# Zero products of a two-layer attention and feed-forward kernel: placed by a weighed sum of the product kinds, issued in four column groups, with new letters for the order

## The chip, the cores and the metric

The kernel runs on one core of a Trainium2 chip. The metric is the device time of one execution in microseconds (us). Several executions are timed; one more is profiled, and its profile gives a span (first to last instruction) and the clock that TensorE was granted.

## What is computed

The reference takes one sequence of 2048 rows of 512 bf16 numbers through two equal layers with shared weights. 32 heads have 16 dimensions each, and the hidden width of the feed-forward part is 1792.

```python
x = A_x
x = x + attention(layernorm(x), A_wqkv, A_wo)      # softmax(q k^T / 4) v, 32 heads of 16, full (no mask)
x = x + silu(layernorm(x) @ B_w1) @ B_w2
x = x + attention(layernorm(x), A_wqkv, A_wo)
x = x + silu(layernorm(x) @ B_w1) @ B_w2
```

## The kernel before

**Tiles and segments.** The attention of a layer is cut into segments: a chunk of 512 queries and a block of four heads (`Seg`). A segment runs over key tiles of 128 keys, and a key tile over two pairs of heads, which makes 2048 tiles in all. TensorE computes the scores of a tile with two matmuls of 32 rows (L1282, in the scores function) into one of three PSUM slots of 128 x 1024. Then one of two engines takes the exponential of the slot:

- ACT does it directly in one instruction of 128 x 1024 (L1497, `act_turn`).
- DVE writes a linear function of the score as 16-bit bits (L1531, `dve_turn`), and three shifted copies of it are made, each by one pass on POOL (L1592, `pool_turn`) or on DVE (L1565). The four together stand for one exponential, so such a tile feeds TensorE four value products instead of one.

The value product (L1358, `values`) has 17 stationary columns (16 dimensions and a column of ones for the sum) and writes into one 32-partition group of the PSUM tile `o_ps`. Two or four of them stand side by side in the array's column groups.

**Side work.** The projections to keys, queries and values, the output projection and the feed-forward part are lists of steps (`Piece`). Their products are issued as four matmuls of 32 columns side by side (L312). The hidden layer's activation is a tanh on ACT (L580) with a DVE instruction behind it (L584). A query tile `QT` needs a chain: the maximum of the keys (L348, L355), a bias matrix `bm` (L412), the absolute query `qu` (L404), one product of the two (L312) and a sum (L421). Without `QT` no scores of its segment can be issued.

**The order.** Everything between the opening and the ending is put in order by a planner that runs while the program is built (`Flow`). It keeps a clock for PE, ACT, DVE and POOL, with fixed durations for each instruction, and gives the next turn to the engine whose clock is earliest. PE has two modes: R for scores, in which the array is split in row groups, and C for values and side work, in which it is split in column groups. Each change between them is planned at 100 ns (`SWITCH`), a product step at 217 ns (`MM`). The engines then run in the recorded order. `due` in the planner says when ACT will need the next scores.

**The letters.** For each stretch of 16 tiles a letter of `RULES` picks seven settings from `KINDS` (`rule`, L977): how many buffers must be free for DVE to take a tile, how many value pairs may wait before they go ahead of side work, at how few free buffers they go anyway, how many shift passes may wait when DVE takes another tile, a factor on the pace of the side work, and from which length of the queue and with which wait DVE helps with passes.

**Zero products.** If PE has nothing to issue that fits ahead of the next scores, `pe_turn` calls `warm` (L1379). Here a matmul of zero weights (16 columns of `wkq` that hold zeros) may be issued. It adds nothing to `o_ps`, or writes into a bank or slot that nobody uses at that time. It is issued only when the share of the last 3300 ns in which PE was planned to stream (`share`, L1375) is at most `WARM`, 0.65, or `HOT`, 0.9, while the next tile has no query tile yet. In mode R it uses 32 rows, in mode C 128 rows, and it always uses one column group. The opening (L1736) and the ending (L660) have zero products of their own.

Of the kernel before, what the change touches and what calls it, by code (L numbers as in the profile page):

```python
# [20 lines left out]
def kernel(  # L21
# [10 lines left out]
    nc = tc.nc  # L32
# [3 lines left out]
    S, D = xf.shape  # L36
    F = B_w1.shape[-1]
    P = 128
    H = 32
    DH = D // H  # L40
# [8 lines left out]
    KR = 32  # L49
# [890 lines left out]
    class Flow:  # L940
# [114 lines left out]
        def step(self, p, at):  # L1055

            engine, ns, fn, g = p.steps.pop(0)
            if not p.begun and p not in self.bg:
                self.cur = p
                for q in self.qs:  # L1060
                    if p in q:
                        q.remove(p)
            p.begun = True
            if p.chain is not None:
                self.chain = p.chain
            self.credit -= ns
            if engine == "pe":
                if self.mode != "C":
                    at += SWITCH
                self.mode = "C"  # L1070
                end = self.pe = at + ns
                self.runs.append((at, end))
                lat = (0, 200, 200)
            elif engine == "dve":
                if "l" in g:
                    at = max(at, self.lock)
                    self.held_port = at + ns
                end = self.dve = at + ns
                lat = (50, 0, 50)
            else:  # L1080
                self.act = max(at + ns, self.end - 446)
                self.end = max(at + ns + 113, self.end + 491)
                end = self.end
                lat = (50, 32, 0)
            fn()
            if p.store is not None and turns:
                p.store.done = True
                p.store.ready = self.landed(end)
            if p.steps:
                p.land = max(p.land, self.landed(end))  # L1090
            if g == "c":
                self.g = end + 50
                self.cur = None
                if p.steps:
                    self.bg.append(p)
            if p.steps:
                p.ready = end + lat[("pe", "dve", "act").index(p.steps[0][0])]
            else:
                p.done = True
                if p.chain is not None and p.chain["last"] is p:  # L1100
                    self.chain = None
                p.ready = max(p.land, self.landed(end), end + 50 + p.lag)
                if p in self.bg:
                    self.bg.remove(p)
# [155 lines left out]
        def scores(self, at, picks):  # L1260

            if self.mode != "R":
                at += SWITCH
            self.mode = "R"
            two = len(picks) == 2
            self.pe = at + (MM + 8 if two else MM + 3)
            self.runs.append((at, at + MM))
            new = []
            for k in picks:
                t = Tile(self.n)  # L1270
                if self.n % STRETCH == 0:
                    self.rule(self.n)
                self.n += 1
                if t.seg.i > self.started:
                    self.started = t.seg.i
                    self.begin(t.seg)
                if t.pr == 0 and t.kt != t.seg.kts[0]:
                    self.pace(t.seg, t.kt - t.seg.kts[0])
                t.slot, t.at = k, at
                for jj in range(2):  # L1280
                    j = 2 * t.pr + jj
                    nc.tensor.matmul(  # L1282
                        self.slots[k][:, jj, :],
                        lhsT=KT[32 * j : 32 * j + KR, t.seg.hb, t.kt * P : (t.kt + 1) * P],
                        rhs=t.seg.QT[32 * j : 32 * j + KR, :],
                        start=True,
                        stop=True,
                    )
                self.held[k] = t
                new.append(t)  # L1290
            if two and len(self.lanes[new[0].pr]) < len(self.lanes[new[1].pr]) - EVEN:
                new.reverse()
            for t in reversed(new):
                if self.want_dve(t, at, two) and not any(x.dve for x in new):
                    t.dve = True
                    self.last_dve = t.n
                    self.zs.append(t)
                    t.bufs = [self.take()] + [None] * (len(SHIFTS) - 1)
            self.exps += sorted((t for t in new if not t.dve), key=lambda t: t.n)
# [43 lines left out]
        def values(self, at, rows):  # L1343

            if self.mode != "C":
                at += SWITCH
            self.mode = "C"
            self.pe = at + MM + 4
            self.runs.append((at, at + MM))
            seg = segs[self.open]  # L1350
            for r in rows:
                _, t, buf, term = r
                pr = t.pr
                self.lanes[pr].remove(r)
                seg.rows[pr] -= 1
                for jj in range(2):
                    j = 2 * pr + jj
                    nc.tensor.matmul(  # L1358
                        self.o_ps[32 * j : 32 * j + VW, :],
                        lhsT=vs[seg.L][:, t.kt, 4 * seg.hb + j, :],  # L1360
                        rhs=buf[:, jj, :],
                        start=not seg.opened[pr],
                        stop=seg.rows[pr] == 0,
                        skip_group_check=True,
                    )
                seg.opened[pr] = True
                t.uses[term] -= 1
                if not t.uses[term]:
                    self.give((self.pe + 150, buf))
            if seg.rows == [0, 0]:  # L1370
                self.close_at = self.pe + 204

        def share(self, t):  # L1375
            self.runs = [r for r in self.runs if r[1] > t - SPAN]
            return sum(b - max(a, t - SPAN) for a, b in self.runs) / SPAN

        def warm(self, t, limit):  # L1379
            idle = self.n < len(tiles) and tiles[self.n][0].QT is None  # L1380
            if t + MM > limit or self.share(t) > (HOT if idle else WARM):
                return False
            if any(segs[self.open].opened) and self.close_at is None:
                out = self.o_ps
            elif self.cur is None and self.g <= t:
                out = narrow("w_ps")
            else:
                slots = [k for k in range(3) if self.held[k] is None and self.free[k] <= t]
                if not idle or not slots:
                    return False  # L1390
                out = self.slots[slots[0]][:, 0, :]
            rows = slice(0, KR if self.mode == "R" else P)
            nc.tensor.matmul(  # L1393
                out[0:DH, :], lhsT=wkq[rows, 0, 2 * D : 2 * D + DH], rhs=wo_sb[rows, 0, :],
                start=out is not self.o_ps, stop=out is not self.o_ps, skip_group_check=True,
            )
            self.pe = t + MM
            self.runs.append((t, self.pe))
            return True


# [57 lines left out]
        def tail(self, t):  # L1459
            if self.n < len(tiles) or not self.units or not self.turned.done:  # L1460
                return False
            tq, k = self.units[0]
            if len(self.kept) <= tq // 2:
                free = [
                    i for i in range(3)
                    if self.held[i] is None and self.free[i] <= t and i not in self.kept
                ]
                if not free:
                    return False
                self.kept.append(free[0])  # L1470
            if self.mode != "C":
                t += SWITCH
            self.mode = "C"
            tail_mm([self.slots[i] for i in self.kept], tq, k)
            self.units.pop(0)
            self.pe = t + MM
            self.runs.append((t, self.pe))
            return True

        def act_turn(self):  # L1480
# [135 lines left out]
    SWITCH, T_PASS, T_BITS, T_SHIFT = 100, 1225, 430, 1000  # L1616

    LAST, ROWS, LATE, EVEN = 5, 20, 900, 0
    SPAN, WARM = 3300, 0.65
    STRETCH = 16  # L1620
    KINDS = {
# [10 lines left out]
    }  # L1632
    RULES = (
        "bbbbbbbbmmmmmmmmwwwwwwwwwwwwwwwwppppppppbbbbbbbbddddddddcccccccc"
        "aaaaaaaakkkkkkkknnnnnnnnvvvvvvvvwwwwwwwwwwwwwwwweeeeeeeellllllll"
    )
    TAU, NEAR, URGENT, HARD = 700, 300, 4000, 6000
    FROM, TO, EARLY = 0, 99, 300
    EARLIER = 12
    SOON, CLOSE = 150, -9999  # L1640
    HOT = 0.9
    MOST = 2600

    OPENING = """
# [6 lines left out]
    at = {}  # L1651
# [142 lines left out]
```

## Time and profile before

| what | value |
|---|---|
| median of 3 runs | 1627.8 us (1621.85, 1627.8, 1628.68) |
| profiled execution | 1620.71 us, of which the span is 1618.9 us |
| mean granted TensorE clock | 0.991 |
| busy PE, DVE, ACT, POOL | 1546.3, 1239.8, 1557.0, 1293.6 us |
| exponentials on ACT, on DVE | 1596, 452 |
| zero products in the trace, L1393 | 211 |

A busy time counts every moment in which at least one instruction of the engine is under way. Matmuls overlap each other in the pipeline, so a PE that is always busy isn't at its peak. Rows of the timeline merge instructions of one kind that follow each other, with their count behind an x. "Idle before" is the time in which the engine did nothing ahead of such a row, with the instruction whose end released it.

### The profile page before, as it was taken

To read this page: it belongs to the slowest core of one execution; us is meant where nothing else is said; L and a number is where in the kernel's file an instruction comes from. 1 tells how busy PE (TensorE), PEld (TensorE's weight loads), DVE (VectorE), ACT (ScalarE), POOL (GpSimd) and SP (SyncE) were. 2 spreads that over 40 slices of the span, in tenths; PEclk is the share of its full clock that TensorE was granted. 3 is DMA by queue.
4 is the path that set the end of the run, shared out by engine and by line. 5 is a ranking of instruction groups with operands and counts; after the bars stand their busy time and mean duration, and the time that the engine had idled before them with its cause. 6 is when DMAs were issued, how large, how long until landed. Compare 5 with 4: busy or idle time off the path is not lost.

```text
span 1618.9 us, 41459 instructions
## 1 busy us (share of the span) xinstructions
PE 1546.3 (96%) x16750; PEld 477.4 (29%) x16756; DVE 1239.8 (77%) x1550; ACT 1557.0 (96%) x1767; POOL 1293.6 (80%) x1349
## 2 busy tenths in 40 slices
PE   8999999999999999999999999998999999999998
PEld 3322222233322323233222232222223222222333
DVE  7898888876777678658987668886878887777764
ACT  6999999999999999999999998998999999999993
POOL 3899998987898778868777866876879998889880
PEclk9999999999999999999999999998999999999999
DMA  5011101100210011001120011112100110010000
GB/s 195 21 40 37 30 23 27 27 11 11 37 23 11 11 27 41 11 14 33 57 59 23 14 27 35 37 35 45 30 11 17 33 27 14 18 33 18 17 24 14
DMA packets 105744, 49.24 MB, mean 30 GB/s; under 512 B 79024, under 2 KB 105040, under 8 KB 105552
## 3 DMA queue, kind: packets, MB, share of 16 engines
q1 hardware_dynamic: 103536, 45.51, 11.0%
q8 instruction: 131, 2.15, 0.6%
q10 hardware_dynamic: 2016, 1.08, 0.2%
q14 instruction: 61, 0.50, 0.1%
HBM read 17.20 MB, written 11.27 MB: 18 GB/s over the span
## 4 chain that ended last, share of the span: by engine, by line
PE 59%; ACT 22%; DVE 11%; issue 6%; POOL 2%; DMA 1%; ACTq 0%; DVEq 0%; POOLq 0%
PE slot L1282 21%; PE q_ps L1358 19%; ACT p L1497 15%; PE y_ps L312 7%; PE h_ps L312 4%; DVE p L1531 3%; ACT v L1497 3%; ACT t_sb L580 2%; PE k_ps L312 2%; PE v_ps L312 1%; PE q_ps L312 1%; POOL p L1592 1%; DVE hT L584 1%; PE w_ps L1393 1%; DVE kq L334 1%
## 5 line engine op out<-in xcount | busy, mean ns | idle before, releaser
L1497 ACT ACTIVATE p<-slot 128x1024 bf16<-128x1024 f32 x1168 | 1172.4, 1203 | 17.4 <-PE slot L1282 17.1
L1592 POOL TENSOR_TENSOR p<-p,steps 128x512 int32<-128x512 int32 x681 | 710.9, 1068 | 186.6 <-DVE p L1531 167.2
L1282 PE MATMUL slot<-QT,KT 32*128 32x512 bf16 x4096 | 596.6, 383 | 36.8 <-ACT p L1497 18.3
L1358 PE MATMUL q_ps<-p,v 128*17 128x512 bf16 x4956 | 566.1, 384 | 5.6 <-DVE p L1531 2.3
L1531 DVE TENSOR_SCALAR p<-slot 128x1024 uint16<-128x1024 f32 x341 | 415.5, 1219 | 106.0 <-PE slot L1282 99.9
L1282 PEld LDWEIGHTS <-KT 32*128 32x128 bf16 x4096 | 198.8, 91 | 615.9 <-issue 609.9
L1497 ACT ACTIVATE v<-slot 128x1024 bf16<-128x1024 f32 x289 | 329.3, 1211 | 1.9 <-PE slot L1282 1.9
L1358 PEld LDWEIGHTS <-v 128*17 128x17 bf16 x6808 | 157.3, 88 | 292.9 <-issue 244.1
L1358 PE MATMUL q_ps<-v,v 128*17 128x512 bf16 x1222 | 195.2, 382 | 1.2 <-POOL v L1592 0.8
L1592 POOL TENSOR_TENSOR v<-p,steps 128x512 int32<-128x512 int32 x159 | 170.4, 1081 | 23.2 <-DVE p L1531 17.1
L1592 POOL TENSOR_TENSOR p<-v,steps 128x512 int32<-128x512 int32 x123 | 130.8, 1081 | 8.4 <-DVE v L1531 8.0
L312 PE MATMUL h_ps<-xnT,w_sb 128*32 128x512 bf16 x1568 | 130.3, 384 | 6.8 <-DVE hT L584 6.6
L312 PE MATMUL y_ps<-w_sb,hT 128*32 128x512 bf16 x1568 | 121.8, 383 | 0.5 <-DVE hT L584 0.5
L584 DVE SCALAR_TENSOR_TENSOR hT<-t_sb,h_ps 128x512 bf16<-128x512 f32 x98 | 66.8, 682 | 58.2 <-ACT t_sb L580 57.9
L1531 DVE TENSOR_SCALAR v<-slot 128x1024 uint16<-128x1024 f32 x69 | 84.2, 1220 | 26.8 <-PE slot L1282 25.7
L1497 ACT ACTIVATE wkq<-slot 128x1024 bf16<-128x1024 f32 x74 | 87.2, 1215 | 0.1
L312 PE MATMUL k_ps<-xnT,wkq 128*32 128x512 bf16 x960 | 78.2, 383 | 0.0
L580 ACT ACTIVATE t_sb<-h_ps 128x512 f32<-128x512 f32 x98 | 76.0, 776 | 0.0
L421 DVE SCALAR_TENSOR_TENSOR QT<-qc,cols,q_ps 128x512 bf16<-128x512 bf16 x74 | 55.0, 743 | 21.6 <-PE q_ps L312 21.0
L1358 PE MATMUL q_ps<-wkq,v 128*17 128x512 bf16 x336 | 58.3, 387 | 0.6 <-ACT wkq L1497 0.4
L312 PEld LDWEIGHTS <-hT 128*32 128x32 bf16 x2016 | 41.0, 95 | 57.1 <-issue 40.8
L1497 ACT ACTIVATE wv_sb<-slot 128x1024 bf16<-128x1024 f32 x44 | 51.7, 1174 | 4.7 <-PE slot L1282 4.5
(168 smaller groups left out, 1469.5 us busy)
## 6 DMA issues: line engine op xcount, KB each, us to landing
qc<-kept_q SPq DMA_DIRECT2D x70, 112.0 KB, 2.0
kept_q<-kq SPq DMA_DIRECT2D x60, 128.0 KB, 1.8
w_sb<-in_B_w_dram SPq DMA_DIRECT2D x2, 1792.0 KB, 13.0
out_dram<-x_sb SPq DMA_DIRECT2D x15, 128.0 KB, 1.7
x_sb<-in_A_x_dram SPq DMA_DIRECT2D x3, 512.0 KB, 7.0
old_q<-QT SPq DMA_DIRECT2D x10, 128.0 KB, 1.7
q_was<-old_q SPq DMA_DIRECT2D x10, 128.0 KB, 2.0
at<-oT SPq DMA_TRANSPOSE x63, 2.3
```

What stands on the lines that cost most here:

```text
L312: nc.tensor.matmul(ps[g, :], lhsT=lhsT[:, g], rhs=rhs, start=start, stop=stop, skip_group_check=True)
L334: nc.vector.tensor_copy(out=st[:], in_=cell["ps"][:, :])
L421: nc.vector.scalar_tensor_tensor(out=dst, in0=qc[:], scalar=own, in1=ps, op0=ALU.mult, op1=ALU.add)
L580: nc.scalar.activation(t_sb, ps, ACT.Tanh, scale=0.5)
L584: nc.vector.scalar_tensor_tensor(out=hT[:, ft, :], in0=t_sb, scalar=1.0, in1=ps, op0=ALU.add, op1=ALU.mult)
L1282: nc.tensor.matmul(self.slots[k][:, jj, :], lhsT=KT[32 * j : 32 * j + KR, t.seg.hb, t.kt * P : (t.kt + 1) * P], rhs=t.seg.QT[32 * j : 32 * ...
L1358: nc.tensor.matmul(self.o_ps[32 * j : 32 * j + VW, :], lhsT=vs[seg.L][:, t.kt, 4 * seg.hb + j, :], rhs=buf[:, jj, :], start=not seg.opened ...
L1393: nc.tensor.matmul(out[0:DH, :], lhsT=wkq[rows, 0, 2 * D : 2 * D + DH], rhs=wo_sb[rows, 0, :], start=out is not self.o_ps, stop=out is not ...
L1497: nc.scalar.activation(buf[:].rearrange("p a b -> p (a b)"), self.slots[x.slot][:].rearrange("p a b -> p (a b)"), ACT.Exp, scale=float(SCALE),
L1531: nc.vector.tensor_scalar(out=whole.bitcast(U16), in0=self.slots[x.slot][:].rearrange("p a b -> p (a b)"), scalar1=float(UNIT), scalar2=fl ...
L1592: nc.gpsimd.tensor_tensor(out=b1.bitcast(I32), in0=b0.bitcast(I32), in1=steps32[:, k : k + 1].to_broadcast([P, 512]), op=ALU.add,)
```

## The change

The planner records for each PE step a weight beside its time: `ANY` plus `SCORE`, `VALUE` or `SIDE` for each product that runs side by side in it. The sum of time by weight over the last 3400 ns (`heat`) takes the place of the share, with the bounds 1.4 (`WARM`) and 2.2 (`HOT`). A zero product is now four matmuls of 128 rows in the four column groups. If PE is in mode R, the planner changes to C first and adds 100 ns; only where that doesn't fit ahead of the next scores does it issue a single one of 32 rows. Last, 21 of the 32 groups of four letters in `RULES` are others.

```diff
-                self.runs.append((at, end))
+                self.runs.append((at, end, ANY + 4 * SIDE))
...
-            self.runs.append((at, at + MM))
+            self.runs.append((at, at + MM, ANY + (4 if two else 2) * SCORE))
...
-            self.runs.append((at, at + MM))
+            self.runs.append((at, at + MM, ANY + 2 * VALUE * len(rows)))
...
-        def share(self, t):
+        def heat(self, t):
             self.runs = [r for r in self.runs if r[1] > t - SPAN]
-            return sum(b - max(a, t - SPAN) for a, b in self.runs) / SPAN
+            return sum((b - max(a, t - SPAN)) * w for a, b, w in self.runs) / SPAN
...
-            if t + MM > limit or self.share(t) > (HOT if idle else WARM):
+            if t + MM > limit or self.heat(t) > (HOT if idle else WARM):
...
-            rows = slice(0, KR if self.mode == "R" else P)
-            nc.tensor.matmul(
-                out[0:DH, :], lhsT=wkq[rows, 0, 2 * D : 2 * D + DH], rhs=wo_sb[rows, 0, :],
-                start=out is not self.o_ps, stop=out is not self.o_ps, skip_group_check=True,
-            )
+            narrowly = self.mode == "R" and t + MM + 2 * SWITCH > limit
+            if self.mode == "R" and not narrowly:
+                t += SWITCH
+                self.mode = "C"
+            rows = slice(0, KR if narrowly else P)
+            for j in range(1 if narrowly else 4):
+                nc.tensor.matmul(
+                    out[32 * j : 32 * j + DH, :], lhsT=wkq[rows, 0, 2 * D : 2 * D + DH],
+                    rhs=wo_sb[rows, 0, :],
+                    start=out is not self.o_ps, stop=out is not self.o_ps, skip_group_check=True,
+                )
             self.pe = t + MM
-            self.runs.append((t, self.pe))
+            self.runs.append((t, self.pe, ANY if narrowly else ANY + 4 * SIDE))
...
-    SPAN, WARM = 3300, 0.65
+    SPAN, WARM = 3400, 1.4
+    ANY, SCORE, VALUE, SIDE = 0.9, 0.27, 0.58, 0.47
...
-        "bbbbbbbbmmmmmmmmwwwwwwwwwwwwwwwwppppppppbbbbbbbbddddddddcccccccc"
-        "aaaaaaaakkkkkkkknnnnnnnnvvvvvvvvwwwwwwwwwwwwwwwweeeeeeeellllllll"
+        "mmmmllllllllllllCCCCCCCCCCCCCCCCmmmmmmmmmmmmBBBBvvvvdddddddddddd"
+        "aaaaaaaakkkkkkkknnnnnnnnddddddddwwwwwwwwwwwwwwwwhhhhyyyynnnnaaaa"
...
-    HOT = 0.9
+    HOT = 2.2
```

More of the change, by code (lines that the diff above doesn't have):

```diff
@@ L1476, in tail @@
             self.pe = t + MM
-            self.runs.append((t, self.pe))
+            self.runs.append((t, self.pe, ANY + 4 * SIDE))
             return True
```

## The prediction

> **What bounds the kernel now.** First the page's busy shares and slices.
>
> ```profile
> PE 1546.3 (96%) x16750; PEld 477.4 (29%) x16756; DVE 1239.8 (77%) x1550; ACT 1557.0 (96%) x1767; POOL 1293.6 (80%) x1349
> ...
> ACT  6999999999999999999999998998999999999993
> ...
> PEclk9999999999999999999999999998999999999999
> ```
>
> PE and ACT are equally busy, so the share doesn't tell which one decides. The timeline does: is one of them issued at a fixed step, without gaps?
>
> ```profile
> 700.31 0.60 ACT L580 ACTIVATE t_sb<-h_ps 128x512 f32<-128x512 f32 x1
> ...
> 700.79 1.04 ACT L1497 ACTIVATE p<-slot 128x1024 bf16<-128x1024 f32 x1
> ...
> 702.59 6.57 ACT L1497 ACTIVATE p<-slot 128x1024 bf16<-128x1024 f32 x7
> ...
> 704.04 1.48 PE L312 MATMUL y_ps<-w_sb,hT 128*32 128x512 bf16 x24
> ```
>
> Seven exponentials take 6.57 us and one takes some 1.06, so one follows the other by (6.57 - 1.06) / 6 = 0.918 us; the tanh takes 0.48 of ACT's order (700.31 to 700.79). ACT's first exponential starts at 31.8 us and the last ends at 1576.5: 1544.7 us. At 0.917 and 0.49, 1596 exponentials, 98 tanh and 10 rescaling exponentials (L493) need 1516.4. So **ACT's order is the bound**: 98 % of the main stretch, and the rest is 28.3 us of pauses. The groups put 24.7 us of idle ahead of L1497 (17.4 + 1.9 + 0.1 + 4.7 + 0.6, by output), nearly all ended by scores from PE; the other 3.6 refill ACT's pipeline. PE matters only where scores are late. Its 24 side products are six steps of four, (1.48 - 0.39) / 5 = 0.218 us each.
>
> The second question is the granted clock. In narrow stretches it is 0.5 in five places and 1.0 elsewhere. The next rows are the five stretches of half clock, the 3.41 us ahead of two of them, and one ordinary stretch; columns are PE, PEld, DVE, ACT, POOL busy, then the clock.
>
> ```profile
> 244.98:248.39 3.41, 3.41 (x26) 0.57 (x28) 1.54 (x2) 2.49 (x4) 2.88 (x4) 0.50 0.02 3
> 599.97:603.38 3.41, 3.41 (x23) 0.47 (x22) 2.55 (x3) 2.78 (x3) 3.13 (x4) 0.50 0.14 32
> 1077.83:1084.66 6.83, 6.30 (x46) 1.15 (x44) 4.34 (x7) 5.19 (x6) 3.03 (x3) 0.50 0.43 58
> 1115.38:1125.62 10.24, 9.32 (x52) 1.80 (x50) 5.90 (x8) 4.91 (x6) 5.87 (x7) 0.50 0.10 24
> 1132.45:1135.86 3.41, 3.41 (x31) 0.82 (x34) 2.94 (x5) 2.92 (x4) 2.53 (x3) 0.50 0.10 34
> ```
> ```profile
> 241.57:244.98 3.41, 3.14 (x22) 0.90 (x20) 1.96 (x3) 3.41 (x5) 3.40 (x4) 1.00 0.16 38
> ...
> 1111.97:1115.38 3.41, 2.15 (x16) 0.60 (x16) 2.76 (x4) 3.41 (x4) 3.41 (x4) 1.00 0.00 0
> ...
> 1202.00:1205.41 3.41, 2.95 (x40) 0.83 (x33) 2.24 (x4) 3.41 (x5) 1.35 (x2) 1.00 0.00 0
> ```
>
> The half clock comes in units of 3.41 us, eight in all, 27.3 us. ACT idles there for 0.92 + 0.63 + 1.64 + 5.33 + 0.49 = 9.0 us; with its share of the refills (28.3 / 24.7) that is 10.3 us. The worst place shows how:
>
> ```profile
> 1120.38 0.75 DVE L421 SCALAR_TENSOR_TENSOR QT<-qc,cols,q_ps 128x512 bf16<-128x512 bf16 x1 [3.41 <-PE q_ps L312]
> ...
> 1121.88 1.02 ACT L1497 ACTIVATE wv_sb<-slot 128x1024 bf16<-128x1024 f32 x1 [3.53 <-PE slot L1282]
> ```
>
> The bias product for the next query tile is late at half clock, so QT is, so are the scores, and ACT stands for 3.53 us.
>
> What precedes a drop? Not an idle PE: 3.14 us of 3.41 are busy at 241.57, more than the 2.95 at 1202. It is the number of products in column groups:
>
> ```profile
> 1111.97:1115.38 3.41, 0.99 (x6) 0.19 (x6) 1.00 0.00 0
> ...
> 1202.00:1205.41 3.41, 1.58 (x18) 0.39 (x11) 1.00 0.00 0
> ```
>
> These are the value products (L1358): 6 against 18. With side products and zero products the five stretches ahead of a drop hold 6 to 15, the one at 1202 holds 30. Cutting the whole main stretch into such windows (a product at an edge by its part), 443 have full clock and a median of 28 column products. Of 8 with under 11, four precede a drop; of 18 with under 14, five; of the rest none. So a low count is necessary here and isn't always enough.
>
> **The change, part by part**, by the recorded orders of both programs.
>
> 1. *Exponentials.* ACT gets 1591 instead of 1596; tanh stay 112 (14 of them in the ending). 5 x 0.917 = **-4.6 us** on the bound. What takes them: DVE has 5 more L1531 (1.22 us each) and 6 more passes L1565 (0.77), POOL 9 more L1592 (1.07): 10.7 us of DVE and 9.6 us of POOL, hidden by their idle shares of 23 and 20 %. Without that cover the late values would hold buffers and delay ACT, by 10.7 us at most.
>
> 2. *Zero products in the flow.* 211 steps become 141: 138 of four products and 3 narrow ones. That frees 70 x 0.217 = 15.2 us of PE. Value steps +14, scores steps -9, side steps -2 cost 0.7; six more mode changes each way cost 12 x 0.10 = 1.2 (scores at 703.72 to products at 704.04 is 0.32, less the step of 0.217). PE's order gets 13.3 us shorter, but it isn't the bound. I take 0. The price of a group of four isn't in the trace: like four side products it is one step of 0.218; at worst its four loads of 16 columns (L1393, 86 ns each) stand in a row, 0.344, and 138 x 0.127 = 17.5 us would lie on PE. I take the first, the nearer row. Behind each stands the next score step or value step, and ACT waits only for the first; 67 of the 141 steps stand right ahead of scores, against 107 of 211 before.
>
> 3. *The clock.* Unknown, with two ends: all eight units go (-10.3), or none (0), or more come (below). What the row says: ahead of the drops stood 4, 3, 2, 0 and 3 zero products. Of two thirds as many steps, each four wide, three become two steps and eight products, so a window of 10 gets to 15, above the 14 under which drops occurred. Laid out along ACT's order (0.917 and 0.49 per instruction), windows of 3.41 us with under 11 column products are about 5 in the order before and 1.5 in the order after; with under 14, 19 and 12. That is 0.3 to 0.65 of the risk left. But the window at 1111.97, which cost the most, had no zero product at all: PE stood waiting there, which the planner didn't foresee. I take half: **-5 us**.
>
> 4. *The letters.* They change which scores go to DVE and when side work runs, so ACT's other pauses (24.7 - 9.0 = 15.7 us idle) are drawn anew. The order shows where scores pause: stretches of at least eight column steps between two score steps are 7 before and 12 after. The longest, at tile 1274, goes from 22 steps to 15; before it is ACT's pause of 4.0 us at 992.5, ended by scores after a wait for QT's chain on DVE, which stays, so I count no gain. A new one of 13 steps stands at tile 1026, and the old one of 12 steps at 1050 (1.1 us idle at 814.9) is down to 8. I take 0, with -4 and +10 as ends.
>
> 5. *The ending.* Two products of the output projection move from the flow into it: 2 x 0.22, half hidden behind ACT's copies: +0.2, ends 0 and 0.4. The opening's order is the same.
>
> The sum: 1620.7 - 4.6 - 5 + 0.2 = **1611.3** for an execution like the profiled one (1620.71, of which 1.8 us lie outside the span). That one is 7 us below the median of 1627.8; the four known times stand as two pairs, near 1621 and 1628, mean 1624.8. Since the program is fixed, I put the spread to how many windows drop (an estimate; one execution can't show it). Some of it stays, +1: I predict **1612**, 1.0 % below the median.
>
> **A rule against it.** The Trainium skill, "TensorE: Matmul & The Clock Gate", section "Part 1: The HAM clock gate (the "warmup" mystery)", says that the clock follows how busy PE was in free-running windows of 3413 ns, and that a window of idleness halves it. The units of 3.41 us agree; the idleness doesn't, for PE is 63 to 92 % busy in the two windows shown ahead of drops. By the rule, groups of four gain no more than single products, and the sum is that of rival B; by the row, it is point 3.
>
> **Rivals.**
>
> - *B: busy time decides, not products; or the drops just move.* Then four side by side count like one, the wider groups do nothing, and 70 fewer steps even hurt. For it: the window at 1111.97 is also low in PE busy (2.15 us of 3.41). Against: 3.14 busy dropped, 2.95 did not. It gives 1620.7 - 4.6 = 1616; with a quarter more units (2 x 10.3 / 8 = 2.6), 1619. The rule above leads here.
> - *C: all units go.* 1620.7 - 4.6 - 10.3 = 1606.
> - *D, slower: the new order starves ACT.* Five more long stretches without scores. ACT holds three slots, 2.75 us; eight steps and two changes are 1.95, so they cost nothing if the slots are full, and up to the 4.0 us of tile 1274 if QT is late. Five at 4.0, with no clock gained, are 1620.7 - 4.6 + 20 = 1636. At 2.5 us each it is 0.5 % above the profiled time (1628.8), at 4.0 each 0.5 % above the median (1635.9). For it: 13 steps at tile 1026. Against: the four 8-step stretches that exist (tiles 448, 1138, 1922, 1952) lie in slices in which ACT is busy for 40.0 of 40 us.
>
> **How the numbers follow.** Half mended 0.42 (1612, its own range 1607 to 1617), C 0.17, B 0.25, D 0.16. A measurement can tell about 0.5 %, 8 us. Faster: the forecast, C, and a quarter of B, 0.65. Same: the rest of B and a quarter of D, 0.23. Slower: 0.12. The range reaches to C with a few us of luck in point 4 (1602) and over B to the mild side of D, 1627.
>
> **What would show it.** Right: ACT's step still 0.917 with 1591 exponentials, half clock in under five units, idle ahead of L1497 near 20 us, groups of four in 0.22 steps. Wrong: eight or more units; or new pauses of over 2 us at tile 1026 (some 794 us in the order before) or near the changed letters; or score steps late behind zero products.

## The result, and the profile after

| | before | after |
|---|---|---|
| median of 22 executions | 1624.32 us (1620.03 to 1629.54) | 1620.21 us (1617.32 to 1622.98) |
| ratio of the times, 95 % interval | | 0.9974 (0.9965 to 0.9984) |
| profiled execution | 1620.71 us (span 1618.9) | 1622.98 us (span 1621.2) |
| mean granted clock | 0.991 | 0.993 |
| exponentials on ACT | 1596 | 1591 |

The change saves 4.1 us, 0.26 % (0.16 to 0.35 %). The forecast was 1612, 8 us lower. The two profiled executions alone would say the opposite, 2.3 us slower: the one of before is near the fastest of its 22, the one of after is the slowest of its 22. So one more execution of before was profiled, and two more of after, and stretches are compared by means over all of them.

From the page of after, the lines that answer to those of before (engines; the granted clock in 40 slices; the two large groups of exponentials, with busy time, mean of one in ns, idle time ahead and its releaser):

```profile
PE 1530.3 (94%) x17118; PEld 482.7 (30%) x17124; DVE 1243.1 (77%) x1561; ACT 1552.8 (96%) x1762; POOL 1301.1 (80%) x1358
...
PEclk9999999999999999999999999999999999999999
...
L1503 ACT ACTIVATE p<-slot 128x1024 bf16<-128x1024 f32 x1206 | 1192.1, 1190 | 24.2 <-PE slot L1282 23.9
...
L1503 ACT ACTIVATE v<-slot 128x1024 bf16<-128x1024 f32 x268 | 298.3, 1186 | 4.9 <-PE slot L1282 3.6
```

(L1497 of before is L1503 here, L1531 is L1537, L1592 is L1598, L1393 is L1398.) PE is busy for 16 us less, where the prediction had its order 13.3 us shorter. That alone is no time won, since ACT's order is the bound. The one slice with an 8 in PEclk (the 28th, 1093 to 1133 us) is gone. Yet the idle time ahead of ACT's exponentials, 24.7 us before, has grown. Where? The view of windows gives ACT's busy time in five stretches (start:end, length, ACT busy and instructions, granted clock, DMA share, GB/s). First before, then after:

```profile
40.00:240.00 200.00, 198.97 (x218) 1.00 0.10 30
240.00:700.00 460.00, 457.03 (x517) 0.99 0.10 21
700.00:960.00 260.00, 258.00 (x289) 1.00 0.12 33
960.00:1140.00 180.00, 164.66 (x183) 0.94 0.16 38
1140.00:1560.00 420.00, 418.54 (x477) 1.00 0.10 22
```
```profile
40.00:240.00 200.00, 189.34 (x206) 0.97 0.10 30
240.00:700.00 460.00, 459.87 (x520) 1.00 0.10 21
700.00:960.00 260.00, 254.91 (x287) 0.99 0.11 32
960.00:1140.00 180.00, 169.15 (x189) 0.98 0.17 39
1140.00:1560.00 420.00, 417.83 (x477) 1.00 0.10 22
```

Length less busy is ACT's idle time. Over the two profiles of before and the three of after, in us:

| stretch | before | after | difference of means |
|---|---|---|---|
| 40 to 240 | 1.0, 1.1 | 10.7, 8.3, 7.6 | +7.8 |
| 240 to 700 | 3.0, 3.2 | 0.1, 0.1, 0.1 | -3.0 |
| 700 to 960 | 2.0, 3.1 | 5.1, 4.2, 4.2 | +2.0 |
| 960 to 1140 | 15.3, 19.2 | 10.9, 9.0, 8.9 | -7.7 |
| 1140 to 1560 | 1.5, 2.4 | 2.2, 2.2, 2.2 | +0.3 |
| sum | 22.8, 28.9 | 28.9, 23.9, 23.0 | -0.6 |
| units of half clock in the main stretch | 8, 12 | 6, 3, 4 | -5.7 |

The three profiles of after have 3, 2 and 2 of their units in the first stretch, those of before none. So the change took 10.7 us of pauses out of two stretches and put 9.8 into two others. With the exponentials (-4.6) and the ending (+0.3: 42.7 us from the last exponential's end instead of 42.4) this is -4.9, against -4.1 measured over 22 executions.

**What came.** The start had no pause of over 0.5 us before. After has these, from the timeline of ACT (start, duration, count behind the x, and in brackets the idle time before), first in its profiled execution, then in the third one:

```profile
73.37 1.94 ACT L1503 ACTIVATE v<-slot 128x1024 bf16<-128x1024 f32 x2 [1.07 <-PE slot L1282]
104.28 1.02 ACT L1503 ACTIVATE p<-slot 128x1024 bf16<-128x1024 f32 x1 [0.84 <-PE slot L1282]
219.48 1.94 ACT L1503 ACTIVATE p<-slot 128x1024 bf16<-128x1024 f32 x2 [1.92 <-PE slot L1282]
...
232.26 1.94 ACT L1503 ACTIVATE v<-slot 128x1024 bf16<-128x1024 f32 x2 [1.53 <-PE slot L1282]
```
```profile
76.17 1.94 ACT L1503 ACTIVATE v<-slot 128x1024 bf16<-128x1024 f32 x2 [1.07 <-PE slot L1282]
...
107.08 1.02 ACT L1503 ACTIVATE p<-slot 128x1024 bf16<-128x1024 f32 x1 [0.84 <-PE slot L1282]
...
220.93 2.05 ACT L1503 ACTIVATE p<-slot 128x1024 bf16<-128x1024 f32 x2 [2.35 <-PE slot L1282]
```

Two kinds of pause can be told apart here. 1.07 and 0.84 come back to the hundredth, 2.8 us later on the clock: they belong to the order. The 1.53 at 232.26 is missing in the third execution (0.53 in the second): it belongs to a unit of half clock that fell there. One profile can't tell the two kinds; several profiles of the same program can in most cases. A pause of a unit can repeat too: a pause of 0.84 us at 225.8 of the third execution stands in the second as well, where units fell on the same instructions, and not in the first.

Behind the pause at 219.48 stands DVE, not PE. From the timeline of all engines:

```profile
212.41 1.27 DVE L321 TENSOR_SCALAR KT<-kq,cols 128x512 bf16<-128x512 bf16 x1
...
216.23 1.21 DVE L348 TENSOR_REDUCE amax<-KT 128x1 f32<-128x1024 bf16 x1
...
217.36 1.21 DVE L1537 TENSOR_SCALAR p<-slot 128x1024 uint16<-128x1024 f32 x1
...
218.62 0.39 PE L1358 MATMUL q_ps<-p,v 128*17 128x512 bf16 x2 [1.87 <-DVE p L1537]
```

The key piece's work on DVE (L321 took 1.27 us here, 0.77 in the mean of its 60) and the maximum (L348) stand ahead of the tile that DVE takes. The value product of that tile stands next in PE's order, so PE waits 1.87 us, and the scores behind it are late by as much for ACT.

**What went.** In the stretch from 960 to 1140 us the pause of 3.53 us that the prediction shows at 1121.88 stood in both profiles of before and in none of after; and the longest one, at tile 1274, is shorter by 1.7 us. About 0.7 of that is one instruction of the chain to `QT`, L321: 1.12 us at 988.24 in before, where POOL worked beside it, and 0.41 at 995.44 in after, where POOL stood. Before, then after:

```profile
992.47 1.02 ACT L1497 ACTIVATE p<-slot 128x1024 bf16<-128x1024 f32 x1 [4.02 <-PE slot L1282]
```
```profile
999.59 1.02 ACT L1503 ACTIVATE p<-slot 128x1024 bf16<-128x1024 f32 x1 [2.36 <-PE slot L1282]
```

### The profile page after: what moved, and what is told of

It reads as the page before. It is cut to its first block, busy times and chain, and to the rows that moved or that the text cites. A ratio compares the mean times of both kernels' runs of the same rounds, so it can differ in the third digit from the quotient of the medians.

```text
span 1621.2 us, 42218 instructions
## 1 busy us (share of the span) xinstructions
PE 1530.3 (94%) x17118; PEld 482.7 (30%) x17124; DVE 1243.1 (77%) x1561; ACT 1552.8 (96%) x1762; POOL 1301.1 (80%) x1358
## 4 chain that ended last, share of the span: by engine, by line
PE 58%; ACT 17%; DVE 12%; POOL 6%; issue 5%; DMA 1%; ACTq 0%; DVEq 0%; POOLq 0%
PE slot L1282 20%; PE q_ps L1358 19%; ACT p L1503 12%; PE y_ps L312 7%; POOL p L1598 4%; PE h_ps L312 4%; PE k_ps L312 3%; DVE p L1537 3%; ACT v L1503 2%; ACT t_sb L580 2%; POOL v L1598 1%; PE v_ps L312 1%; DVE hT L584 1%; PE q_ps L312 1%; DVE attn L514 1%
## 5 line engine op out<-in xcount | busy, mean ns | idle before, releaser
L1503 ACT ACTIVATE p<-slot 128x1024 bf16<-128x1024 f32 x1206 | 1192.1, 1190 | 24.2 <-PE slot L1282 23.9
L1598 POOL TENSOR_TENSOR p<-p,steps 128x512 int32<-128x512 int32 x658 | 687.3, 1068 | 174.5 <-DVE p L1537 134.1
L1282 PE MATMUL slot<-QT,KT 32*128 32x512 bf16 x4096 | 587.7, 383 | 46.7 <-ACT p L1503 25.6
L1358 PE MATMUL q_ps<-p,v 128*17 128x512 bf16 x4994 | 561.9, 383 | 10.9 <-DVE p L1537 4.0
L1537 DVE TENSOR_SCALAR p<-slot 128x1024 uint16<-128x1024 f32 x331 | 403.8, 1220 | 115.6 <-PE slot L1282 101.8
L1503 ACT ACTIVATE v<-slot 128x1024 bf16<-128x1024 f32 x268 | 298.3, 1186 | 4.9 <-PE slot L1282 3.6
L1358 PEld LDWEIGHTS <-v 128*17 128x17 bf16 x6838 | 164.1, 88 | 292.5 <-issue 239.4
L1598 POOL TENSOR_TENSOR v<-p,steps 128x512 int32<-128x512 int32 x161 | 172.0, 1074 | 27.7 <-DVE p L1537 18.8
L1598 POOL TENSOR_TENSOR p<-v,steps 128x512 int32<-128x512 int32 x127 | 132.8, 1064 | 16.7 <-DVE v L1537 7.4
L312 PE MATMUL y_ps<-w_sb,hT 128*32 128x512 bf16 x1568 | 118.0, 382 | 0.1
L1537 DVE TENSOR_SCALAR v<-slot 128x1024 uint16<-128x1024 f32 x72 | 87.9, 1221 | 31.2 <-PE slot L1282 28.7
L1503 ACT ACTIVATE wkq<-slot 128x1024 bf16<-128x1024 f32 x55 | 66.3, 1223 | 0.1
L1598 POOL TENSOR_TENSOR v<-v,steps 128x512 int32<-128x512 int32 x48 | 51.8, 1086 | 10.4 <-DVE v L1537 9.9
## 6 DMA issues: line engine op xcount, KB each, us to landing
w_sb<-in_B_w_dram SPq DMA_DIRECT2D x2, 1792.0 KB, 12.6
```

The costliest lines, as they stand in the source:

```text
L312: nc.tensor.matmul(ps[g, :], lhsT=lhsT[:, g], rhs=rhs, start=start, stop=stop, skip_group_check=True)
L1282: nc.tensor.matmul(self.slots[k][:, jj, :], lhsT=KT[32 * j : 32 * j + KR, t.seg.hb, t.kt * P : (t.kt + 1) * P], rhs=t.seg.QT[32 * j : 32 * ...
L1358: nc.tensor.matmul(self.o_ps[32 * j : 32 * j + VW, :], lhsT=vs[seg.L][:, t.kt, 4 * seg.hb + j, :], rhs=buf[:, jj, :], start=not seg.opened ...
L1503: nc.scalar.activation(buf[:].rearrange("p a b -> p (a b)"), self.slots[x.slot][:].rearrange("p a b -> p (a b)"), ACT.Exp, scale=float(SCALE),
L1537: nc.vector.tensor_scalar(out=whole.bitcast(U16), in0=self.slots[x.slot][:].rearrange("p a b -> p (a b)"), scalar1=float(UNIT), scalar2=fl ...
L1598: nc.gpsimd.tensor_tensor(out=b1.bitcast(I32), in0=b0.bitcast(I32), in1=steps32[:, k : k + 1].to_broadcast([P, 512]), op=ALU.add,)
```

## The experiments

The theory after the result: the clock gain came about as forecast, and the new letters' own pauses took it back. The first rival (theory P of the expectations): the clock hardly moved, and five exponentials fewer are the whole 4.1 us. The second rival, B of the prediction: four products side by side do no more than one. Theory W is its opposite: the width keeps the clock. Each expectation says what its theories give. All ratios are to the kernel before on the same chip, with a 95 % interval.

**Placement without the letters, and letters without the placement.** The first is the kernel after with the letters of before (198 groups of four, 1595 exponentials on ACT):

```diff
-        "mmmmllllllllllllCCCCCCCCCCCCCCCCmmmmmmmmmmmmBBBBvvvvdddddddddddd"
-        "aaaaaaaakkkkkkkknnnnnnnnddddddddwwwwwwwwwwwwwwwwhhhhyyyynnnnaaaa"
+        "bbbbbbbbmmmmmmmmwwwwwwwwwwwwwwwwppppppppbbbbbbbbddddddddcccccccc"
+        "aaaaaaaakkkkkkkknnnnnnnnvvvvvvvvwwwwwwwwwwwwwwwweeeeeeeellllllll"
```

> The changed kernel with the letters of before: zero products placed by the weighed sum and four side by side (198 groups of four and 2 narrow ones in the flow), 1595 exponentials on ACT against 1596 before and 1591 after. Theory P (places and order: the gain is five fewer exponentials, the clock hardly moves, since it drops where PE stands and waits and no zero product can be issued): within 2 us of before, ratio 0.999 to 1.001. Theory W (width: four products keep the clock, and the letters lose part of that again): 4 us or more below before, ratio 0.9975 or less, with fewer than 5 units of half clock of 3.41 us.

Measured: 1640.83 us, ratio 1.0101 (1.0080 to 1.0122). The second is the kernel before with the new letters, the reverse of this diff (289 single zero products, 1597 exponentials):

> The kernel before with the new letters alone: 289 single zero products by share of time, 1597 exponentials on ACT. By itself the planner gives it no fewer exponentials, so theory P expects no gain, ratio 0.999 to 1.002. Theory L (the new letters are the better order whatever the zero products do) expects the 4 us of the whole change, ratio 0.9975.

Measured: 1661.28 us, 1.0233 (1.0209 to 1.0257). Each half alone is slower, by 16 and 37 us, and the two together are 4 faster. All theories missed both times: none had expected more than 1.002. Nothing in the work changed by much; the order did. In the first kernel two pauses hold 27 us. One of them, from its timeline:

```profile
998.02 0.69 DVE L379 CAST v<-v_ps 128x512 bf16<-128x512 f32 x1 [1.15 <-PE v_ps L312]
...
1002.45 1.05 PE L312 MATMUL k_ps<-xnT,wkq 128*32 128x512 bf16 x16
...
1004.29 2.69 PE L1398 MATMUL w_ps<-wo_sb,wkq 128*16 128x512 bf16 x24 [0.36 <-DVE kq L334]
...
1005.63 0.29 DVE L412 TENSOR_SCALAR bm<-E,amax 128x128 bf16<-128x128 f32 x1
...
1007.04 0.40 PE L312 MATMUL q_ps<-qu,bm 128*32 128x512 bf16 x4
...
1008.78 1.94 ACT L1503 ACTIVATE p<-slot 128x1024 bf16<-128x1024 f32 x2 [14.86 <-PE slot L1282]
```

When the next segment's first tile was due, its value pieces, its last key piece and the chain to `QT` were still to be done; ACT stood for 14.86 us while PE and DVE took turns at them. Zero products had a small part: six groups of four went ahead of the chain's product, which began at 1007.04 though its bias matrix was ready at 1005.92. A product takes 0.38 us, so these six groups into the narrow bank `w_ps` follow each other by (2.69 - 0.38) / 5 = 0.46 us, over twice the planner's 0.217. Two groups into `q_ps`, the trace's name for `o_ps`, follow by 0.60 - 0.38 = 0.22, here in after:

```profile
992.96 0.60 PE L1398 MATMUL q_ps<-wo_sb,wkq 128*16 128x512 bf16 x8
```

The two runs fit the reading that letters suit only the placement that they were chosen with: a letter sets the pace of the side work, and a step more or less in the flow moves which piece is unfinished at a change of segment. They don't test it further.

**Width and number of the zero products, in each order.** In the new order the planner is left as it is, and one product of each group of four, or none, is issued:

```diff
-            for j in range(1 if narrowly else 4):
+            for j in range(1):
```

> The order of the changed kernel to the instruction, but of each group of four zero products only the first is issued (141 zero products instead of 555). Only the width differs from the changed kernel. Theory P: within 1.5 us of it, so ratio to before 0.9965 to 0.9985, 5 to 8 units of half clock. Theory W: the units rise to 10 or more and the time by 4 us or more above the changed kernel, ratio 1.000 or more.

```diff
-            for j in range(1 if narrowly else 4):
+            for j in range(0):
```

> The order of the changed kernel, but none of the zero products of the flow is issued (those of the opening and the ending stay). It measures what zero products are worth at all. Theory P: they stand mostly where the clock would stay anyway, so 0 to 4 us above the changed kernel, ratio to before 0.997 to 1.000. Theory W: 8 us or more above the changed kernel, ratio 1.002 or more, with 12 or more units of half clock.

And in the order of before, four in place of one in mode C (then none at all, with the matmul of `warm` left out):

```diff
-            nc.tensor.matmul(
-                out[0:DH, :], lhsT=wkq[rows, 0, 2 * D : 2 * D + DH], rhs=wo_sb[rows, 0, :],
-                start=out is not self.o_ps, stop=out is not self.o_ps, skip_group_check=True,
-            )
+            for j in range(1 if self.mode == "R" else 4):
+                nc.tensor.matmul(
+                    out[32 * j : 32 * j + DH, :], lhsT=wkq[rows, 0, 2 * D : 2 * D + DH],
+                    rhs=wo_sb[rows, 0, :],
+                    start=out is not self.o_ps, stop=out is not self.o_ps, skip_group_check=True,
+                )
```

> The order of the kernel before to the instruction, with its letters, but each zero product issued in column mode is four side by side (157 of the 211; the 54 of 32 rows stay single). Theory P, after the run with one of four in the changed order (the same as with four): width is worth nothing, ratio 0.998 to 1.001. Theory W: with the old places the width shows after all, ratio 0.9975 or less.

> The order of the kernel before, but none of the 211 zero products of the flow is issued. If the two orders differ only by their five exponentials (4.6 us), this is 3 to 6 us above the changed order without zero products (ratio 1.0043), so 1.006 to 1.009 to before. If the changed order's places are what the zero products need, this costs clearly less than the 9.6 us that they were worth there, ratio 1.000 to 1.004.

The second profile of before, and two more of after, the last of them timed too, were taken to tell fixed pauses from those of the clock:

> The kernel before once more, for a second profile: 1596 exponentials at 0.917 us in both. If the spread between executions (1620 to 1630 us) is the clock and the pauses it causes, a time away from 1620.7 comes with another number of units of half clock, about 0.5 us for each; the pauses at the fixed places (tiles 1050 and 1274) stay.

> The changed kernel once more, for a second profile. The first profiled execution, 1623.0 us, was near the slowest of its 22. If pauses with fixed places (tiles 252, 1027, 1051, 1274, 1851) are the order's, they return at the same tiles and within 0.3 us; units of half clock differ and carry the difference in time.

> The changed kernel again, timed on the chip of the other runs of this call: 1620 us, ratio 0.997 to 0.998, and a third profile of it. It tells whether the runs with one of four (1618.6) and with four in the old order (1620.9) differ from it by more than two chips do.

They took 1627.74, 1617.22 and 1618.60 us in their profiled executions; the last has a median of 1619.96. And the kernel with one of four again:

> The order of the changed kernel with one of the four zero products, again, on the chip on which the changed kernel is timed in the same call. If width is worth nothing in this order: within 1.5 us of it. If four products keep the clock better here too: 2 us or more above it.

| order | zero products | median us | ratio | units of half clock, by profile | mean granted clock of the timed executions |
|---|---|---|---|---|---|
| before | none | 1623.43 | 1.0004 (0.9986 to 1.0022) | 13 | 0.982 (12) |
| before | one (the kernel before) | 1624.32 | 1 | 8, 12 | 0.989 (91) |
| before | four | 1620.90 | 0.9971 (0.9956 to 0.9986) | 3 | 0.993 (12) |
| after | none | 1629.79 | 1.0043 (1.0021 to 1.0065) | 23 | 0.978 (9) |
| after | one | 1618.59, 1619.35 | 0.9967 (0.9951 to 0.9983), 0.9971 (0.9956 to 0.9985) | 8, 5 | 0.995 (24) |
| after | four (the kernel after) | 1620.21, on a second chip 1619.96 | 0.9974 (0.9965 to 0.9984), 0.9976 (0.9961 to 0.9992) | 6, 3, 4 | 0.994 (34) |

The last column has the number of executions in brackets. A unit is about 0.001 of the mean clock, so the column counts units over many executions, where a profile counts those of one.

In the old order single zero products bought no time that could be measured, within the lower of the two expected ranges, though they raised the clock from 0.982 to 0.989. At one and the same clock, 0.985, the order without them took 1621.0 and 1621.3 us, the kernel before on the same chip 1628.6 and 1628.7. So either zero products cost time themselves, or the units that they keep away are cheap ones; no run separates the two. Four in the same places bought 3 us more and a clock of 0.993, as much as the whole change within the intervals. In the new order zero products are needed, for without them it loses 9.6 us, as theory W had it, but one per place is as good as four, in time and in clock. Four have about 2 us more of pauses in the first 240 us; why, was not examined. Against the second rival, width can count; against the theory's simple form, effects of width and order don't add up.

The price of a unit comes from two executions of the same program: before with 12 units had 6.1 us more ACT idle than with 8, 1.5 us per unit, and took 7.0 us longer (1627.74 against 1620.71). In after, 6 units against 3 cost 5.0 of idle. Over the 91 executions of before whose clock is listed, the time rises by 1.1 us for each unit of lost clock (correlation 0.92), over the 34 of after by 1.0. The expectation of 0.5 us was too low; that the spread of a kernel's executions is mostly its units, as the prediction estimated, is borne out.

**Where do the pauses at the start come from?** If the letters make them, the first letters of before must take them away. Letters alone were changed in four kernels, on top of the kernel after; strings were drawn until the planner's own clock was short. The first changes the end instead, the second the start and the end:

```diff
-        "aaaaaaaakkkkkkkknnnnnnnnddddddddwwwwwwwwwwwwwwwwhhhhyyyynnnnaaaa"
+        "aaaaaaaakkkkkkkknnnnnnnnddddddddwwwwwwwwwwwwwwwwCCCCCCCCnnnnllll"
```

> The changed kernel with other letters from tile 1792 on (CCCCCCCCnnnnllll in place of hhhhyyyynnnnaaaa); the order up to there is the same. 1588 exponentials instead of 1591. If the time is ACT's order plus pauses that belong to places in the order: 3 x 0.917 = 2.8 us below the changed kernel, about 1617.5, with the same pauses up to 1350 us. If what a changed kernel gains in exponentials comes back as pauses, it is no faster than the changed one, 1620.

```diff
-        "mmmmllllllllllllCCCCCCCCCCCCCCCCmmmmmmmmmmmmBBBBvvvvdddddddddddd"
-        "aaaaaaaakkkkkkkknnnnnnnnddddddddwwwwwwwwwwwwwwwwhhhhyyyynnnnaaaa"
+        "bbbbbbbbmmmmmmmmCCCCddddCCCCaaaammmmmmmmmmmmBBBBvvvvdddddddddddd"
+        "aaaaaaaakkkkkkkknnnnnnnnddddddddwwwwwwwwwwwwBBBBBBBByyyyllllllll"
```

> The changed kernel with the letters of before for tiles 0 to 255 and others of our own choice behind them (found with the planner); 1589 exponentials. In both profiles of the changed kernel ACT pauses for 12 to 15 us in the first 240 us, in both of the kernel before for 4.1. Theory A (those pauses come from the new letters at the start): 4 to 6 us of pauses there, and 1610 to 1614 us in all. Rival (they come from where zero products go, or any new order draws as many): 10 us or more of pauses there, and 1618 us or more.

Measured: 1623.36 us, 1.0001 (0.9985 to 1.0017), and 1629.51 us, 1.0028 (1.0013 to 1.0044), both slower than after and far from the times that the theory gave. The start of the second was mended, as the theory says: 3.5 us of waits for scores in the first 240 us against 12.6 in after (view of waits). But from ACT's last exponential to the end of the span it took 56.4 us, and the first kernel 49.7, instead of 42.7. The second kernel's timeline shows what filled that:

```profile
1571.17 3.21 PE L312 MATMUL y_ps<-w_sb,hT 128*32 128x512 bf16 x56 [0.95 <-DVE x_sb L593]
...
1574.43 0.69 DVE L593 SCALAR_TENSOR_TENSOR x_sb<-y_ps,x_sb 128x512 bf16<-128x512 f32 x1 [3.31 <-PE y_ps L312]
```

Feed-forward pieces of 3.21 us, left over by the flow, run one after the other with nothing beside them. The letters had been chosen by the planner's time at the last tile, which doesn't see them. With the left-over work counted, two others were chosen:

```diff
-        "mmmmllllllllllllCCCCCCCCCCCCCCCCmmmmmmmmmmmmBBBBvvvvdddddddddddd"
+        "bbbbbbbbmmmmmmmmCCCCCCCCllllllllllllmmmmmmmmBBBBvvvvdddddddddddd"
```

> The changed kernel with the letters of before for tiles 0 to 255, others of our own for tiles 256 to 703 and those of the changed kernel from 704 on; 1593 exponentials, and no more side work left for the ending than in the changed kernel (which the run with the first letters of before had: its ending took 56.4 us instead of 42.7). Theory A (the pauses of the first 240 us belong to the new letters there, 11.5 to 15.1 us in three profiles): they are 4 to 5 us here, which is -7 to -10, and two more exponentials +1.8: 1612 to 1616 us, ratio 0.992 to 0.995. Rival (what is saved at the start comes back elsewhere): 1619 us or more, with over 24 us of pauses behind 240 us.

```diff
-        "mmmmllllllllllllCCCCCCCCCCCCCCCCmmmmmmmmmmmmBBBBvvvvdddddddddddd"
-        "aaaaaaaakkkkkkkknnnnnnnnddddddddwwwwwwwwwwwwwwwwhhhhyyyynnnnaaaa"
+        "bbbbbbbbmmmmmmmmCCCCddddCCCCaaaammmmmmmmmmmmBBBBvvvvdddddddddddd"
+        "aaaaaaaakkkkkkkknnnnnnnnddddddddwwwwwwwwmmmmmmmmhhhhhhhhyyyycccc"
```

> The same test on another order: the letters of before for tiles 0 to 255 and another set of our own behind (1593 exponentials, 42 to 43 us of ending). Theory A: 4 to 5 us of pauses in the first 240 us, and 1612 to 1618 us, since the pauses behind it are drawn by the order and were 15 to 22 us in the three profiles of the changed kernel. Rival: 1619 us or more.

Measured: **1617.44 us, 0.9950 (0.9932 to 0.9968), and 1617.09 us, 0.9946 (0.9928 to 0.9964)**: both are faster than before, and some 3 us faster than after, whose interval (0.9965 to 0.9984) just touches theirs. The second lies in the range of its theory A, the first 1.4 us above it. The windows of the first of the two:

```profile
40.00:240.00 200.00, 198.53 (x217) 1.00 0.12 31
240.00:700.00 460.00, 459.67 (x521) 1.00 0.09 21
700.00:960.00 260.00, 252.10 (x283) 0.98 0.12 31
960.00:1140.00 180.00, 171.87 (x191) 1.00 0.17 40
```

The start is back at 1.5 us of idle, 7.4 less than after's mean, and so it is in all three kernels with the first letters of before: those letters do make the pauses. But from 700 to 960 us it now idles 7.9 instead of 4.5, where three units of half clock fell in its profile, and ACT has two more exponentials (1593). The net is -3 us, and the time of the first kernel missed its expectation by that return.

## Why the prediction was wrong

The sign was right, the size was not: -4.1 us of the forecast -12 to the median that the 22 executions give (1624.3). The letters' pauses took back most of it, and the clock's gain came without the reason that was given for it. By its own points:

1. *Exponentials, -4.6:* right. 1591 on ACT; their step, where ACT doesn't wait, is 0.915 us in the mean, 0.916 before, and the busy times of DVE and POOL rose by 3 and 8 us without delaying ACT in sum.
2. *Zero products in the flow, 0 on PE:* right for most, with a price that was missed. A group of four that writes into `o_ps` or a slot is one step, the lower of the two ends: in the trace of after, where one such group follows another at once, the second starts 0.215 to 0.220 us behind the first (18 pairs at full clock), and scores start 0.32 behind a group at the earliest, a step and a change of mode. Groups into the narrow bank `w_ps` follow each other only by 0.46 us (17 pairs), above the upper end of 0.344: each starts some 0.07 us behind the end of the one before. PE's busy time fell by 16 us all the same. That fewer zero products are worth nothing in time is not settled: see the two executions at a clock of 0.985.
3. *The clock, -5:* the size came out about right, the reason did not. Against the eight units of the profiled execution, after has 4.3 in the mean of three profiles; 3.7 units at 1.1 to 1.5 us are 4.1 to 5.5. The worst place, at 1122 us, is gone. But the prediction expected this from four products side by side, and in the new order one per place keeps the clock as well (0.995 against 0.994). That the forecast met the number is partly luck. The new places are the likelier cause: the letters of before have a clock of 0.994 with them (and four products) and 0.990 without, the new letters 0.994 and 0.983. No run has the new places and single products with the letters of before, so the cause stays open.
4. *The letters, 0 with ends of -4 and +10:* **this is the step that failed.** The prediction laid out where scores pause by counting steps in PE's order, found tile 1026, and took the rest to be drawn anew with no net. What the runs show in its place is about +8: +7.8 at the start and +2.0 from 700 to 960 us, less 1.7 at tile 1274. Some 2.6 of it are the 2.3 units of half clock, at 1.1 us, that fell at the start in the mean; without them about +5.5 is left. The prediction counted a gain of nothing at tile 1274 and never looked at the start, where before had almost no pause left (1.0 us idle in 200) and a new order could only lose. A count of PE's steps also can't see a pause like the one at 219.48, in which PE waits for DVE. With 5.5 to 8 in place of 0 the forecast of 1612 becomes 1617.5 to 1620; 1620.2 was measured.
5. *The ending, +0.2:* right, +0.3.

The baseline was guessed well: the profiled execution is 3.6 us under the median of 22, and the median of the three runs first shown was 3.5 above it. Of the rivals, C (all units go) fell: 3 to 6 are left. B's price, 1616 to 1619, was nearest the time, and part of it held: in the new order four do count like one, and how much PE streams sorts the drops (below). Against it, units halved, and in the old order width alone gave 0.9971. D named its place rightly. From the timeline of after:

```profile
799.72 1.94 ACT L1503 ACTIVATE p<-slot 128x1024 bf16<-128x1024 f32 x2 [2.19 <-PE slot L1282]
```

This is tile 1027, 2.19 us, within the price that D gave a stretch; there were fewer of them, and others that it hadn't named. The first rival after the result (exponentials alone) fits the sum of -4.1 by chance: its other clause, that the clock hardly moves, fell.

## What to carry to other kernels

When an order is drawn anew, price its pauses stretch by stretch on the engine that bounds the time, and look hardest where that engine hardly idles now: such a stretch can only lose. Profile the same program twice; pauses that don't repeat belong to the clock, those that do mostly to the order, and only then compare two programs. Count lost clock over all executions: the units of one profile put one product per place behind four here, and 24 executions don't. Constants tuned for a planner fit that planner alone (each half of this change was slower, by 16 and 37 us), and a criterion for choosing new ones must count the work that is left over at the end.

## What the runs showed of the hardware

**What comes ahead of a drop of the clock.** Over 16 profiles, 7120 windows of 3.41 us between ACT's first and last exponential had full clock, and 74 of them were followed by half clock. Counting each matmul as its step of 0.217 us from its start, the share of a window in which any product streams tells nearly all:

| share streaming | under 0.40 | 0.40 to 0.50 | 0.50 to 0.60 | 0.60 to 0.65 | 0.65 and more |
|---|---|---|---|---|---|
| windows | 27 | 86 | 401 | 509 | 6097 |
| followed by half clock | 27 | 29 | 16 | 2 | 0 |

The number of column products, one at an edge by its part, sorts them about as well (under 8: 21 of 24; 17 and more: 0 of 6610); both fall together. So the prediction's "not an idle PE" was a misreading of a view: a busy time counts the overlapped tails of matmuls. The window at 241.57, 3.14 us busy, streams for 0.65 of its time, and the one at 1111.97 for 0.44. In after, the window ahead of the drop at 220.21 (columns PE, PEld, DVE, ACT, POOL busy, clock):

```profile
216.80:220.21 3.41, 1.59 (x16) 0.47 (x15) 2.80 (x4) 1.49 (x2) 1.56 (x2) 1.00 0.00 0
220.21:223.62 3.41, 3.16 (x28) 1.05 (x26) 2.48 (x5) 3.04 (x4) 3.41 (x4) 0.50 0.00 0
```

It streams for a third. In all three profiles of after a unit falls at this pause, so the pause pays twice. That streaming alone decides is not shown: in the old order four products in the place of one stream no longer, and gave a clock of 0.993 instead of 0.989.

The Trainium skill, "TensorE: Matmul & The Clock Gate", section "Why this matters for your kernels", advises to leave PE no idle gaps of over some 3 us. The trace is stricter: the longest wait of PE ahead of the drop at 220.21 is 1.87 us, and ahead of the one at 244.98 in before it is 0.2. The Trainium skill, "Perfetto Trace Analysis", section "Identifying the Most-Contended Engine", warns that a matmul busy share doesn't tell how fully PE is used, because its instructions are pipelined. The trace agrees: 92 % busy at 241.57, 65 % streaming.

**One DVE instruction, two durations.** L321 (128x512, bf16) took from 0.40 to 1.29 us in after, against 0.30 in the planner: 0.41 in each of the 7 during which POOL stood, 0.87 in the mean of the 42 that lay beside POOL's work for all of their time (0.40 to 1.27). A planner with fixed durations places such a tile wrongly by more than a product step. That POOL is the cause was not tested by itself.
